# One array width for float32 products: products in halves, zero-filled tiles, paired heads and later-planned DMA consumers in an attention and FFN kernel

## The chip, the cores and the metric

The kernel runs on one core of a Trainium2 chip. The metric is the time on the device in microseconds (us). TensorE is PE in the rows, VectorE is DVE, ScalarE is ACT, GpSimd is POOL, and SyncE (SP) issues all DMAs here.

## The reference

Block-causal attention over 8 batches and 8 heads of 576 tokens and 64 dimensions; the heads side by side (512 columns) go through a feed-forward network (FFN) of 2048 hidden units.

```python
scores = scale * np.matmul(q, k.transpose(0, 1, 3, 2))
mask = pos[:, None] // 64 >= pos[None, :] // 64
scores = np.where(mask, scores, -1e9)
attn = softmax(scores)                       # rows
x = np.matmul(attn, v).transpose(0, 2, 1, 3).reshape(4608, 512)
h = x @ w_in                                 # 512 x 2048
g = h * np.clip(h + 3.0, 0.0, 6.0) / 6.0
out = g @ w_out                              # 2048 x 512
```

## The kernel before

q, k and v arrive as float32. The weights arrive as float64, seen as pairs of 32-bit words; they are made float32 on the chip (`w_load`), then scaled and split into a high and a low float16 part (`w_split`, tiles `win` and `wout`). Most products run on such pairs: high by high, high by low, low by high.

Two heads form a slot `n`; 32 slots, four for each batch. Blocks of 64 queries form groups `g` of three. TensorE's array of 128x128 is used in two widths. Float16 products are written as two halves of 64 output partitions (`h` = 0 and 1), each on 64 columns of the array, which run side by side ("128*64" in the rows, rows by columns of the array in use). Float32 products and all transposes take the whole width ("128*128").

The first batch (slots 0 to 3) has a path of its own in float32, which needs no scales:

- `qk_prep32` transposes q and k on TensorE (`qf`, for the last 192 tokens `qr`, into PSUM tiles `qt`), and lays q out so that one product gives the scores of both heads.
- `s_block32` makes the scores of a block (`sf`), takes their maximum (`st`) and the exponential (`pf` in SBUF); `t_block32` transposes that (`pt`) and copies it into `pT`.
- `pv_group32` spreads the reciprocal sums over the partitions with a product (`pr`, weights `halves`) and multiplies by V (`pf` in PSUM, from `vnat`), one head in each half of the array.
- `ffn1_f32` and the branch `pc == 0` of `ffn2_` are the float32 FFN of the first 384 tokens: `h0_f` and `o0_t`, for 16 hidden tiles f and three row tiles t.

`pow2_scale` finds a power of two over all partitions: it transposes the maxima (`mt`), reduces them, spreads the result over a small diagonal (`dg`) and multiplies by ones (`mb`). Maxima of V (`mt_v`) and of the weights (`mt_w`) take that path. In several places a tile has 64 rows or fewer: the last tokens of a slot in `qr`, the last block of a group in `pt` and `pT`, the last `j` of P V, and `dg` with one or two rows.

The order of all engines is made when the program is built. `Recorder` takes down every operation with a key (a planned time from tables such as `AS`, `RT`, `AT`, `FT`), its tiles and its possible engines (`scaled` lists them: A is ACT, V is DVE, P is POOL). `schedule` simulates the engines from a cost model and takes at each step, among the operations that are ready, the one with the lowest key. For TensorE an operation is `half` or not, and the planner keeps to one width while it can; a change of width costs `TURN`. `joint` keeps instructions together as one operation. `emit` then writes the operations in that order; all of them go through one line of the source (L470), so the rows of the profile are told apart by tile names. Nothing of the plan's times is in the program: an engine waits only for data and free tiles.

```python
            op.half = eng == "tensor" and outs[0].ap[0][1] <= 64 and method == "matmul"
```

Of the kernel before, what the change touches and what calls it, by code (L numbers as in the profile page):

```python
# [10 lines left out]
F32 = mybir.dt.float32  # L11
# [14 lines left out]
U = 1.598  # L26
AS = (7.023, 12.523, 17.83, 23.72)
AL = 18.177
PV0 = 2.73
TA, TR, PR = 2.293, 5.661, 0.564  # L30
QR = 2.65
PVA, PVB = 0.915, 0.993
# [6 lines left out]
EVP = 1  # L39
# [4 lines left out]
QL = -1.069  # L44
VL = -0.957
W0, WD = 22.454, 2.893
S0, SD = 55.334, 3.899
M0, MD = 34.048, 7.213
RT = (32.208, 42.3, 52.129, 62.298)
RS, RL, VL1 = 2.174, 27.037, 23.187  # L50
VM0, VMX = 40.792, 0.335
AT = ((4, 86.25), (6, 128.63), (8, 163.76), (9, 178.32), (10, 200.19), (12, 240.58), (14, 288.15), (16, 335.0), (24, 568.52), (32, 811.01))
FT = ((0, 34), (1, 120), (2, 165.14), (3, 234.43), (4, 274.43), (5, 349.43), (7, 498.87), (10, 739.05), (13, 984.05))
UNI = False
QP = 0.55
VP = 0.469
# [5 lines left out]
class Op:  # L62
# [3 lines left out]
    __slots__ = ("ways", "key", "preds", "joint", "n", "start", "end", "tiles", "eng", "half", "queue")  # L66
# [15 lines left out]
ADV = {("tensor", "a"): 99.36}  # L82


class Recorder:
# [76 lines left out]

    def add(self, ways):
# [56 lines left out]
    def cost(self, eng, method, args, kw, outs, ins):  # L220
# [46 lines left out]
        occ = max(n / 2.37, 26) * (4 if f32 else 1) + 2  # L267
        if f32 and method == "matmul":
            occ = max(occ, 200)
# [6 lines left out]
    def schedule(self):  # L276
# [63 lines left out]
        while done < N:  # L340
# [38 lines left out]
            else:  # L379
# [4 lines left out]
                for i, (key, k, rd) in enumerate(a):  # L384
                    h = ops[k].half
                    if not h and False in first:
                        continue
                    r = room(ops[k], t, full)
                    if r is None:
                        first.setdefault(h, i)  # L390
# [48 lines left out]
            margin = {}  # L439
            if o.queue:  # L440
                lead, tail, work = o.queue
                dma = max(t + lead, dma) + work
                o.end = dma + tail
                margin = self.MARGIN
            now[e] = t + occ
            self.busy[e] += occ
            for x in o.tiles:
                left[x] -= 1
                if not left[x]:
                    tag = self.meta[x][0]  # L450
                    free[tag].append(o.end + 60.0)
                    need[tag][head:span[x][1]] -= 1
# [21 lines left out]
def kernel(  # L474
# [65 lines left out]
    def pow2_scale(mx, n, nm, to=None, exact=False):  # L540
# [8 lines left out]
        if exact:  # L549
            pt_ = ps_s.tile([P, 512], F32, tag="s", name=f"mt_{nm}")  # L550
            nc.tensor.transpose(pt_[:n, :P], mx, ident)
            dg = sm.tile([P, n + 1], F32, tag=f"dg{n}", name=f"dg_{nm}")
            nc.vector.tensor_reduce(dg[:n, n:], pt_[:n, :P], axis=AX.X, op=ALU.max)
            nc.vector.tensor_scalar_mul(dg[:n, :n], ident[:n, :n], dg[:n, n:])
            mx, k_ = dg[:n, :n], n
        else:
            k_ = P
        ps = ps_s.tile([P, 512], F32, tag="s", name=f"mb_{nm}")
        nc.joint = "mb", nm
        for h in range(2):  # L560
            nc.tensor.matmul(ps[h * BLK:(h + 1) * BLK, :n], ones[:k_, :BLK], mx, start=True, stop=True)
# [261 lines left out]
    def qk_load32_rest(n):  # L823
        t = attp.tile([P, 2, NTR, 2, D], F32, tag="vhl", bufs=2, name=f"qr{n}")
        for s, src in enumerate((q, k)):
            nc.sync.dma_start(t[:, s, 0], src[0, 2 * n:2 * n + 2, T0:T0 + P].rearrange("h p d -> p h d"))
            nc.sync.dma_start(
                t[:BLK, s, 1], src[0, 2 * n:2 * n + 2, T0 + P:].rearrange("h p d -> p h d")
            )
        qn[n] = t  # L830

    def qk_prep32(n, rest):
# [28 lines left out]
        pss = []  # L861
        for s in (1, 0):
            if rest and not QTH:
                ps = ps_s.tile([P, 512], F32, tag="s", name=f"qt{n}_{s}r")
            else:
                ps = ps_h.tile([P, T0], F32, tag="h", name=f"qt{n}_{s}")
            for u in range(NTR if rest else NTA):
                m = min(P, c1 - c0 - u * P)
                nc.tensor.transpose(
                    ps[:, u * P:u * P + m], t[:m, s, u].rearrange("p h d -> p (h d)"),  # L870
                    ident[:m, :m],
                )
            pss.append(ps)
        nc.scaled(kT[:, c0:c1], pss[0][:, :c1 - c0], 1.0, "AV")
# [15 lines left out]
    def s_block32(n, i):  # L890
# [39 lines left out]
    def t_block32(n, i):  # L930
# [5 lines left out]
        half = nk % P and ii == GB - 1  # L936
# [10 lines left out]
        for u0 in range(0, nu, 4):  # L947
            u1 = min(u0 + 4, nu)
            full = u1 - 1 if half and u1 == nu else u1
# [5 lines left out]
            for u in range(u0, u1):  # L955
                m = P if u < full else BLK
                nc.tensor.transpose(pp[:m, u - u0], pr[:, u * P:u * P + m], ident)
            for a, e, m in ((u0, full, P), (full, u1, BLK)):
                if a < e:
                    dst = t[:m, ii * NU[g] + a:ii * NU[g] + e]  # L960
                    src = pp[:m, a - u0:e - u0]
                    nc.scaled(dst, src, 1.0, "AV")
            n_ev.append(1)

    def pv_group32(n, g):
# [16 lines left out]
        nc.tensor.matmul(pr, halves, rd.rearrange("p i x -> p (i x)"), start=True, stop=True)  # L982
# [7 lines left out]
        for j in range(nj):  # L990
            i0 = max(0, 2 * j - 3 * g)
            kp = BLK if 2 * j + 1 > 3 * g + 2 else P
            a = i0 * NU[g] + j
            us = slice(a, a + (GB - 1 - i0) * NU[g] + 1, NU[g])
            for h in range(2):
                nc.tensor.matmul(
                    ps[h * D:(h + 1) * D, i0 * BLK:],
                    vnat[n % NVB][:kp, j, h, :],
                    t[:kp, us, h * BLK:(h + 1) * BLK],
                    start=(j == 0),  # L1000
                    stop=(j == nj - 1),
                )
        if g < G32:
# [513 lines left out]
```

## Time and profile before

| | us |
|---|---|
| median of 3 runs | 1009.13 (1006.89 to 1009.73) |
| profiled execution | 1009.89 |
| its span | 1008.1 |
| PE busy | 988.0 (98%) |
| DVE busy | 765.2 (76%) |
| ACT busy | 691.5 (69%) |
| POOL busy | 23.7 (2%) |

The span runs from the first to the last instruction of the profiled execution. The granted clock of TensorE is 0.999 of full speed. Rows of operations in order of time give a start and a length; the length of a product holds a tail in which the next one already runs, so distances between starts tell what a product costs.

### The profile page before, as it was taken

What the parts mean: (1) busy time and instruction counts of PE and PEld (TensorE: products, weight loads), DVE (VectorE), ACT (ScalarE), POOL (GpSimd) and SP (SyncE); (2) the same over time, 40 slices, a digit from 0 to 9 for tenths busy, and PEclk for the clock granted to TensorE, in tenths of its full rate; (3) what the DMA queues carried; (4) which work ended last, traced back from release to release, by engine and by line L of the source; (5) the groups of instructions that cost most, each with busy time, mean ns of one, the idle gap of its engine ahead of it and who ended that gap; (6) DMA issues with size and microseconds to landing.
All of it is one profiled execution on the core that took longest, in us unless ns stands there. A gap on an engine that the chain in (4) does not pass through costs nothing. (4 is left out here: it accounts for less than half of the span.)

```text
span 1008.1 us, 28569 instructions
## 1 busy us (share of the span) xinstructions
PE 988.0 (98%) x11492; PEld 712.6 (71%) x11492; DVE 765.2 (76%) x2107; ACT 691.5 (69%) x1821; POOL 23.7 (2%) x98
## 2 busy tenths in 40 slices
PE   7999999999999999999999999999999999999998
PEld 5655544777767777777667767776777777777776
DVE  5899989899999899989999899689797532333332
ACT  5889876778878787888888787688776432333332
POOL 2000100000000000000000000000000000000000
PEclk9999999999999999999999999999999999999999
DMA  6786756989899888998899887778455300000000
GB/s 151 207 246 206 187 111 123 173 156 173 151 173 188 144 154 172 154 190 161 155 181 179 158 172 150 129 138 150 81 109 97 59 33 1 1 33 2 33 2 33
DMA packets 414197, 128.87 MB, mean 128 GB/s; under 512 B 403184, under 2 KB 403440, under 8 KB 414064
## 3 DMA queue, kind: packets, MB, share of 16 engines
q1 hardware_dynamic: 414064, 127.05, 64.2%
q8 instruction: 90, 1.47, 0.6%
q14 instruction: 43, 0.35, 0.1%
HBM read 45.09 MB, written 9.44 MB: 54 GB/s over the span
## 5 line engine op out<-in xcount | busy, mean ns | idle before, releaser
L470 PE MATMUL h<-x,win 128*64 128x384 f16 (+2 forms) x4720 | 440.0, 317 | 3.7 <-DVE r L470 2.8
L470 PE MATMUL o<-wout,g 128*64 128x512 f16 (+2 forms) x3348 | 432.4, 379 | 0.0
L470 PEld LDWEIGHTS <-win 128*64 128x64 f16 x4608 | 289.1, 110 | 71.7 <-issue 7.4
L470 PEld LDWEIGHTS <-g 128*64 128x64 f16 x3264 | 213.0, 110 | 96.1 <-DVE g L470 0.4
L470 ACT ACTIVATE r<-h,eg,sh 128x192 f32<-128x192 f32 (+1 forms) x240 | 134.2, 580 | 122.8 <-PE h L470 120.1
L470 DVE SCALAR_TENSOR_TENSOR r<-r,eg,h 128x384 f32<-128x384 f32 (+1 forms) x192 | 110.5, 576 | 133.9 <-ACT r L470 133.5
L470 ACT ACTIVATE p<-s,st,esc 128x64 f32<-128x64 f32 (+1 forms) x280 | 163.4, 587 | 16.4 <-DVE ph L470 6.4
L470 DVE SCALAR_TENSOR_TENSOR g<-r,g 128x384 f16<-128x384 f32 (+1 forms) x192 | 99.6, 520 | 34.7 <-ACT g L470 33.7
L470 DVE TENSOR_REDUCE st<-s 128x1 f32<-128x64 f32 (+1 forms) x280 | 117.7, 447 | 7.8 <-PE s L470 7.4
L470 ACT ACTIVATE g<-r 128x384 f16<-128x384 f32 (+1 forms) x151 | 74.3, 492 | 61.6 <-DVE r L470 60.8
L470 PE MATMUL s<-qkT 128*64 128x64 f16 (+7 forms) x1120 | 100.0, 288 | 3.5 <-ACT p L470 1.6
L470 PEld LDWEIGHTS <-qkT 128*64 128x64 f16 x1120 | 58.8, 110 | 35.7 <-issue 17.0
L470 PEld LDWEIGHTS <-vhl 128*64 128x64 f16 x1680 | 72.7, 110 | 14.4 <-issue 7.7
L470 PE MATMUL pv<-pT,vhl 128*64 128x192 f16 (+2 forms) x1680 | 73.8, 233 | 2.0 <-ACT p L470 0.8
L470 DVE SCALAR_TENSOR_TENSOR ph<-p,st,ph 128x256 f16<-128x256 f32 (+2 forms) x168 | 67.4, 445 | 0.0
L470 DVE SCALAR_TENSOR_TENSOR phl<-p,st,phl 128x512 f16<-128x512 f32 (+1 forms) x84 | 62.6, 789 | 0.0
L470 ACT ACTIVATE st<-st,esc 128x1 f32<-128x1 f32 (+2 forms) x127 | 36.7, 291 | 34.5 <-DVE st L470 33.6
L470 ACT ACTIVATION_READ_ACCUMULATOR p<-s,st,esc 128x1 f32 x280 | 55.1, 197 | 0.0
L470 ACT ACTIVATE ph<-p,st 128x192 f16<-128x192 f32 (+5 forms) x102 | 43.6, 468 | 7.4 <-DVE st L470 4.9
L470 ACT ACTIVATE qks<-qk 128x576 bf16<-128x576 f32 x56 | 37.9, 680 | 11.5 <-DMA qkT<-qks 11.5
L470 DVE SCALAR_TENSOR_TENSOR qks<-qk,rs_q,qks 128x576 f16<-128x576 f32 x56 | 43.7, 809 | 0.0
L470 DVE TENSOR_REDUCE vmax<-vnat 128x1 f32<-128x640 f32 x32 | 25.9, 808 | 5.7 <-DMA vnat<-in_v_dram 5.7
(158 smaller groups left out, 836.5 us busy)
## 6 DMA issues: line engine op xcount, KB each, us to landing
out_dram<-osb SPq DMA_DIRECT2D x35, 256.0 KB, 2.7
vnat<-in_v_dram SPq DMA_DIRECT2D x64, 128.0 KB, 2.9
qk<-in_q_dram SPq DMA_DIRECT2D x28, 288.0 KB, 3.6
qk<-in_k_dram SPq DMA_DIRECT2D x28, 288.0 KB, 4.2
rawi<-in_moe_w_in_dram SPq DMA_DIRECT2D x8, 512.0 KB, 4.5
rawo<-in_moe_w_out_dram SPq DMA_DIRECT2D x8, 512.0 KB, 4.5
ph<-in_moe_w_in_dram SPq DMA_DIRECT2D x6, 512.0 KB, 4.6
ph<-in_moe_w_out_dram SPq DMA_DIRECT2D x6, 512.0 KB, 4.1
```

Of the source, the lines that this page charges most:

```text
L470: getattr(eng, method)(*args, **kw)
```

## The change

- A new call `product` records a float32 product once, with a second form (`alt`): two halves of 64 output partitions, written one after the other. Its width is open (`half` is None), and the planner takes the form of the width that TensorE is in. `s_block32`, `pr`, `h0` and `o0` use it.
- Tiles of 64 rows become whole with zeros: `pr` in SBUF has 640 columns, whose tail POOL sets to zero; `t_block32` transposes and copies whole tiles; P V always takes 128 rows of V (whose tail is zero). The rest of q and k is loaded as three tiles, the middle one half q and half k, and gives three transposes in one PSUM bank instead of four in two.
- `mt` is a product in two halves (the maxima as weights, repeated over 64 columns, by the identity) instead of a transpose, and `dg` and `mb` use all 128 partitions.
- The two heads of a step of P V are one operation (`joint`).
- The planner's model (its unit is ns): changes of width cost 92 to half and 120 to full, with 95 more for an operation that begins a visit to full width; consumers of a DMA on every engine are planned 900 later (1250 on TensorE as before), a tile that a DMA frees comes free 900 later, results that TensorE uses come 100 later; unit costs of products are set anew. The tables of keys are new.

```diff
-MARGIN = {"tensor": 1250.0}
+LATE = {"tensor": 100.0}
+MARGIN = {"tensor": 1250.0, "vector": 900.0, "scalar": 900.0, "gpsimd": 900.0, "sync": 900.0}
+SLACK = 900.0
-TURN = 95
+TURN = {True: 92.0, False: 120.0}
+LOADS = 95.0
...
+    def product(self, out, w, x, **kw):
+        self.add([("tensor", "matmul", (out, w, x), kw)])
+        r = BLK
+        op = self.ops[-1]
+        op.half = None
+        op.alt = [
+            ("matmul", (out[h * r:(h + 1) * r], w[:, h * r:(h + 1) * r], x), kw) for h in range(2)
+        ]
...
-            if e == "tensor" and o.half != half:
-                half = o.half
-                self.turns += 1
-                t += self.TURN
+            if e == "tensor":
+                if o.half is None:
+                    if half:
+                        o.ways[e] = o.alt, occ, took, shared
+                elif o.half != half:
+                    half = o.half
+                    self.turns += 1
+                    t += self.TURN[half]
+                    if not half:
+                        occ += self.LOADS
+                        took += self.LOADS
...
-            margin = {}
+            margin, slack = self.LATE, 60.0
...
-                margin = self.MARGIN
+                margin, slack = self.MARGIN, 60.0 + self.SLACK
...
-                    free[tag].append(o.end + 60.0)
+                    free[tag].append(o.end + slack)
...
-            nc.tensor.transpose(pt_[:n, :P], mx, ident)
+            nc.joint = "mt", nm
+            for h in range(2):
+                wide = mx[:, h % n:h % n + 1].to_broadcast([P, BLK])
+                nc.tensor.matmul(pt_[h * BLK:(h + 1) * BLK, :P], wide, ident, start=True, stop=True)
+            nc.joint = None
...
-            kp = BLK if 2 * j + 1 > 3 * g + 2 else P
...
+            nc.joint = "pf", n, g, j
             for h in range(2):
                 nc.tensor.matmul(
                     ps[h * D:(h + 1) * D, i0 * BLK:],
-                    vnat[n % NVB][:kp, j, h, :],
-                    t[:kp, us, h * BLK:(h + 1) * BLK],
+                    vnat[n % NVB][:, j, h, :],
+                    t[:, us, h * BLK:(h + 1) * BLK],
...
-            nc.tensor.matmul(
+            nc.product(
                 ps, w_f32("i", c, d // 2)[:, d % 2, l], x32[:, d, :T0], start=(d == 0), stop=(d == NDT - 1)
             )
...
+                nc.product(a, g[:, c0:c1], w32, start=first, stop=last)
...
-RT = (32.208, 42.3, 52.129, 62.298)
+RT = (29.488, 39.58, 49.409, 59.423)
```

What stands where now. First TensorE about 13 us into the kernel before: scores of slot 1 (`sf1`), P V of slot 0 (`pf0_0` from `pT0` and `vnat0`), transposes (`pt0`, `pt1`), the spread sums (`pr0`). The last numbers are output partitions by columns; x2 is two equal instructions in a row. Before:

```order
L470 MATMUL pf0_0_151<-pT0_0_117,vnat0_100 64x192
L470 MATMUL sf1_0_0_134<-qkf1_124 128x128
L470 MATMUL sf1_1_0_141<-qkf1_124 128x128
L470 MATMUL pt0_4_0_152<-ident_91,pf0_4_138 128x128 x2
L470 MATMUL pr0_0_149<-rd0_0_148,halves_97 128x192
L470 MATMUL pt0_4_0_152<-ident_91,pf0_4_138 128x128
L470 MATMUL pf0_0_151<-pT0_0_117,vnat0_100 64x192
```

With the change:

```order
L491 MATMUL pf0_0_152<-pT0_0_117,vnat0_100 64x192 x2
L491 MATMUL sf1_0_0_134<-qkf1_124 64x128 x2
L491 MATMUL sf1_1_0_141<-qkf1_124 64x128 x2
L491 MATMUL pr0_0_150<-rd0_0_149,halves_97 64x192 x2
L491 MATMUL pf0_0_152<-pT0_0_117,vnat0_100 64x64 x2
L491 MATMUL pt0_4_0_155<-ident_91,pf0_4_138 128x128 x3
```

The two heads of `pf0_0` stand together; the scores and the spread sums behind them are in halves of 64 partitions, and the transposes come in a group after them.

TensorE in the middle of the float32 FFN: `h0` and `o0`, scores `sf3` of the first batch, maxima of the weights (`mt_w`, `mb_w`). Before:

```order
L470 MATMUL h0_6_477<-x0_81,win_85 128x384 x2
L470 MATMUL sf3_7_0_472<-qkf3_0_200,qkf3_2_202 128x512
L470 MATMUL sf3_8_0_481<-qkf3_0_200,qkf3_2_202 128x320
L470 MATMUL mt_w4_465<-ident_91,wm4_463 2x128
L470 MATMUL h0_6_477<-x0_81,win_85 128x384
L470 MATMUL o0_2_396<-wout_86,g0_3_393 128x512
L470 MATMUL sf3_8_1_482<-qkf3_0_200,qkf3_2_202 128x256
L470 MATMUL o0_0_394<-wout_86,g0_4_419 128x512
L470 MATMUL o0_1_395<-wout_86,g0_4_419 128x512
L470 MATMUL mb_w4_467<-dg_w4_466,one_98 64x2 x2
L470 MATMUL h0_7_489<-x0_81,win_85 128x384
```

With the change:

```order
L491 MATMUL mt_w4_484<-ident_91,wm4_482 64x128 x2
L491 MATMUL o0_1_394<-wout_86,g0_4_427 64x512 x2
L491 MATMUL o0_2_395<-wout_86,g0_4_427 64x512 x2
L491 MATMUL pr3_2_499<-rd3_2_498,halves_97 64x192 x2
L491 MATMUL mb_w4_486<-dg_w4_485,one_98 64x2 x2
L491 MATMUL h0_8_531<-x0_81,win_85 64x384 x4
L491 MATMUL mt_w5_514<-ident_91,wm5_512 64x128 x2
L491 MATMUL h0_8_531<-x0_81,win_85 64x384 x4
L491 MATMUL o0_0_393<-wout_86,g0_5_461 64x512 x2
L491 MATMUL mb_w5_516<-dg_w5_515,one_98 64x2 x2
```

Where products of 128 partitions took turns with `mb_w` of 64, everything is of 64 partitions, `mt_w` too.

DVE where the weights of one chunk are split: `rsio` holds the scales, a TENSOR_SCALAR on `win` makes the high part, a SCALAR_TENSOR_TENSOR on `win` with `rsio` the low one. Before:

```order
L470 TENSOR_SCALAR rsio_90<-pwio_89 128x2
L470 TENSOR_TENSOR rb1_2_408<-pf1_2_409,rb1_2_408 128x192
L470 RECIPROCAL rsio_90<-rsio_90 128x2
L470 TENSOR_SCALAR sgi5_0_469<-rawi5_0_468 128x512
L470 TENSOR_SCALAR win_85<-win_85,rsio_90 128x2x256
L470 SCALAR_TENSOR_TENSOR x1_82<-rb1_2_408,rs_v0_207,x1_82 128x192
L470 TENSOR_REDUCE st2_7_413<-sf2_7_0_414 128x1
```

With the change:

```order
L491 TENSOR_SCALAR rsio_90<-pwio_89 128x2
L491 SCALAR_TENSOR_TENSOR win_85<-exi5_0_430,sgi5_0_429 128x512
L491 SCALAR_TENSOR_TENSOR wout_86<-exo3_1_370,sgo3_1_369 128x512
L491 RECIPROCAL rsio_90<-rsio_90 128x2
L491 TENSOR_REDUCE st3_6_450<-sf3_6_0_451 128x1
L491 SCALAR_TENSOR_TENSOR win_85<-win_85,rsio_90 128x2x256 x2
L491 TENSOR_SCALAR sgi4_0_376<-ph1_88 128x512
```

The high parts stand on ACT or POOL there, and DVE makes the two low parts one after the other. In all, DVE makes 1 high part of `win` and `wout` (11 before), ACT 23 (16) and POOL 8 (5).

More of the change, by code (lines that the diff above doesn't have):

```diff
@@ L24 @@
 WY = 27
[L26 to L32, printed above, removed]
+U = 1.592
+AS = (6.899, 12.918, 18.225, 24.115)
+AL = 17.759
+PV0 = 2.584
+TA, TR, PR = 2.701, 5.502, 1.15
+QR = 2.616
+PVA, PVB = 1.013, 0.991
 PHS = 18
@@ L38 @@
 EVR = 3
-EVP = 1
+EVP = 4
 PRO = True
@@ L62 @@
 class Op:
-    __slots__ = ("ways", "key", "preds", "joint", "n", "start", "end", "tiles", "eng", "half", "queue")
+    __slots__ = ("ways", "key", "preds", "joint", "n", "start", "end", "tiles", "eng", "half", "queue", "alt")
 class Engine:
@@ L266, in cost @@
         f32 = mybir.dt.size(ins[0].dtype) == 4
-        occ = max(n / 2.37, 26) * (4 if f32 else 1) + 2
+        occ = max(n / 2.4, 26) * (4 if f32 else 1) + (5 if f32 else 2.7)
         if f32 and method == "matmul":
-            occ = max(occ, 200)
+            occ = max(occ, 90 if n <= 2 else 200)
         if method == "transpose":
@@ L385, in schedule @@
                     h = ops[k].half
-                    if not h and False in first:
+                    if not h and False in first and (h is False or True in first):
                         continue
@@ L389, in schedule @@
                     if r is None:
-                        first.setdefault(h, i)
+                        for m in (True, False) if h is None else (h,):
+                            first.setdefault(m, i)
                         if h:
@@ L823, in qk_load32_rest @@
     def qk_load32_rest(n):
[L824 to L829, printed above, removed]
+        t = attp.tile([P, 3, 2, D], F32, tag="vhl", bufs=2, name=f"qr{n}")
+        for dst, src, t0, t1 in (
+            (t[:, 0], q, T0, T0 + P), (t[:BLK, 1], q, T0 + P, S),
+            (t[BLK:, 1], k, T0, T0 + BLK), (t[:, 2], k, T0 + BLK, S),
+        ):
+            nc.sync.dma_start(dst, src[0, 2 * n:2 * n + 2, t0:t1].rearrange("h p d -> p h d"))
         qn[n] = t
@@ L860, in qk_prep32 @@
         c0, c1 = (T0, S) if rest else (0, T0)
[L861 to L865, printed above, removed]
-                ps = ps_h.tile([P, T0], F32, tag="h", name=f"qt{n}_{s}")
[L867 to L874, printed above, removed]
+        if rest:
+            ps = ps_s.tile([P, 512], F32, tag="s", name=f"qt{n}_r")
+            for u in range(3):
+                nc.tensor.transpose(ps[:, u * P:(u + 1) * P], t[:, u].rearrange("p h d -> p (h d)"), ident)
+            pss = ps[:, GT:2 * GT], ps[:, :GT]
+        else:
+            pss = []
+            for s in (1, 0):
+                ps = ps_h.tile([P, T0], F32, tag="h", name=f"qt{n}_{s}")
+                for u in range(NTA):
+                    nc.tensor.transpose(
+                        ps[:, u * P:(u + 1) * P], t[:, s, u].rearrange("p h d -> p (h d)"), ident
+                    )
+                pss.append(ps)
+        nc.scaled(kT[:, c0:c1], pss[0], 1.0, "AV")
         i, ie = c0 // BLK, c1 // BLK
@@ L955, in t_block32 @@
             for u in range(u0, u1):
[L956 to L962, printed above, removed]
+                nc.tensor.transpose(pp[:, u - u0], pr[:, u * P:(u + 1) * P], ident)
+            nc.scaled(t[:, ii * NU[g] + u0:ii * NU[g] + u1], pp[:, :u1 - u0], 1.0, "AV")
             n_ev.append(1)
@@ L981, in pv_group32 @@
             pr = ps_s.tile([P, GT], F32, tag="s", name=f"pr{n}_{g}")
-        nc.tensor.matmul(pr, halves, rd.rearrange("p i x -> p (i x)"), start=True, stop=True)
+        nc.product(pr, halves, rd.rearrange("p i x -> p (i x)"), start=True, stop=True)
         rb = sm.tile([P, GT], F32, tag="rb", bufs=2, name=f"rb{n}_{g}")
@@ L1295, in ffn2_ @@
                 w32 = w_f32("o", f // 2, f % 2).rearrange("p r l n -> p (r l n)")
-                if c1 - c0 == P:
-                    nc.tensor.matmul(a, g[:, c0:c1], w32, start=first, stop=last)
-                    continue
-                for h in range(2):
-                    nc.tensor.matmul(
-                        a[h * BLK:(h + 1) * BLK, :DM // 2], g[:, c0:c1],
-                        w32[:, h * DM // 2:(h + 1) * DM // 2], start=first, stop=last,
-                    )
+                nc.product(a, g[:, c0:c1], w32, start=first, stop=last)
                 continue
```

45 lines of the change are left out of this document (21 added, 24 removed).

## Prediction

> **What bounds the kernel now.** I read the page's first lines, then busy time by stretches, then TensorE's waits.
>
> ```profile
> span 1008.1 us, 28569 instructions
> PE 988.0 (98%) x11492; PEld 712.6 (71%) x11492; DVE 765.2 (76%) x2107; ACT 691.5 (69%) x1821; POOL 23.7 (2%) x98
> ```
>
> TensorE is busy 988.0 us of 1008.1; no other engine is near that.
>
> ```profile
> core 0: us, PE busy (x) PEld busy (x) DVE busy (x) ACT busy (x) POOL busy (x), PEclk, DMA share, GB/s
> 0.00:60.00 60.00, 52.82 (x287) 34.89 (x288) 43.96 (x137) 43.31 (x133) 9.89 (x37) 1.00 0.72 191
> 60.00:140.00 80.00, 80.00 (x394) 42.16 (x393) 77.40 (x218) 68.52 (x172) 5.81 (x8) 1.00 0.73 193
> 140.00:200.00 60.00, 59.71 (x639) 35.38 (x639) 51.52 (x160) 41.79 (x115) 0.77 (x5) 1.00 0.79 141
> 200.00:650.00 450.00, 442.30 (x6092) 334.30 (x6089) 412.02 (x1172) 361.94 (x1000) 6.05 (x40) 1.00 0.91 165
> 650.00:1008.00 358.00, 353.19 (x4093) 265.85 (x4087) 180.27 (x424) 175.91 (x403) 1.21 (x8) 1.00 0.27 54
> ```
>
> The columns are the stretch and its length, then busy us of PE, weight loads, VectorE (DVE), ScalarE (ACT) and GpSimd (POOL). PE idles 7.2 us in the first 60 us, then not at all up to 140 us. From 200 to 650 us it idles 7.7 us. DVE is nearly as full as PE between 60 and 140 us: 77.4 of 80.
>
> ```profile
> PE qt L470 <- DMA qf<-in_q_dram: 4.2, 1, 4.2
> PE h L470 <- DVE r L470: 2.8, 3, 1.5
> PE s L470 <- ACT p L470: 1.6, 2, 0.8
> PE s L470 <- DVE am_q L470: 1.5, 1, 1.5
> ```
>
> The longest wait of PE is the first load, which the change leaves. Everything else is a few short waits, so what counts is how long PE's own stream is, and "busy" hides gaps between instructions. The order of instructions in time shows those:
>
> ```profile
> 121.01 2.74 PE L470 MATMUL o<-wout,g 128*128 128x512 f32 x6
> 123.59 0.27 PE L470 MATMUL mt_w<-ident,wm 128*2 128x128 f32 x1
> 123.70 2.75 PE L470 MATMUL h<-x,win 128*128 128x384 f32 x8
> 126.28 1.88 PE L470 MATMUL o<-wout,g 128*128 128x512 f32 x4
> ...
> 169.38 0.93 PE L470 MATMUL h<-x,win 128*64 128x192 f16 x18
> 170.25 1.12 PE L470 MATMUL o<-x,g 128*128 128x512 f32 x2
> 171.30 0.44 PE L470 MATMUL h<-x,win 128*64 128x192 f16 x6
> 171.67 1.12 PE L470 MATMUL o<-x,g 128*128 128x512 f32 x2
> ```
>
> The columns are start, length (the last tail included), operation, count. A float32 product is two records here. Three products of 128x512 on the full array take 123.59 - 121.01 = 2.58 us, 0.86 each; the four of 128x384 that follow `mt` take 126.28 - 123.70 = 2.58, 0.645 each, or 0.16 per pass and 192 columns. Between products on half the array (128*64) one takes 171.30 - 170.25 = 1.05, so 0.19 more. The half-array work pays too: 18 halves take 0.87 and six take 0.37, so a pair costs 0.50/6 = 0.083 and 0.12 is left over at the change of width. Going to full width and back for a float32 product costs **0.31 us**.
>
> ```profile
> 65.23 0.60 PE L470 MATMUL pt<-ident,pf 128*128 128x128 f32 x4
> 65.67 0.48 PE L470 MATMUL qt_1r<-ident,qr 128*128 128x128 f32 x2
> 66.07 1.12 PE L470 MATMUL o<-wout,g 128*128 128x512 f32 x2
> ...
> 283.85 0.27 PE L470 MATMUL mt_v<-ident,vm 128*1 128x128 f32 x1
> 284.05 0.84 PE L470 MATMUL o<-wout,g 128*64 128x512 f16 x6
> ```
>
> Four transposes of 128 rows take 0.44, 0.11 each. The two of `qt_1r`, of which one has 64 rows, take 0.40 where 0.22 would do: going to fewer rows and back costs 0.18 as well, 0.09 each way. The transpose `mt_v` takes 0.20 when half-array work follows, against 0.11 for `mt_w` above: 0.09 for the way back, so 0.12 + 0.09 = 0.21 for a visit that begins with transposes.
>
> **The change part by part.** Changes of width or rows, counted in PE's order of both kernels: 160 before, 21 after. Of the 160, 120 are width and 40 rows alone; after it none is rows alone. Visits to full width that begin with a float32 product fall from 41 to none. I divide at the second tile of the first hidden layer (`h0_1`, near 60 us) and at the last `o0` (near 174 us).
>
> *Up to 60 us:* width changes 34 to 12, 11 visits fewer: 8 x 0.31 + 3 x 0.21 = 3.1 us; row changes 11 x 0.09 = 1.0. Heads of P V:
>
> ```profile
> 20.73 0.54 PE L470 MATMUL pf<-pT,vnat 128*64 128x192 f32 x2
> 21.20 0.33 PE L470 MATMUL pt<-ident,pf 128*128 128x128 f32 x1
> ```
>
> A head alone takes 21.20 - 20.73 = 0.47, less 0.09 for the change of width 0.38. A pair shares the array, as the next rows show, and needs two passes of 0.16 = 0.32 for both. Five pairs are split before and none after: 5 x 0.32 = 1.6. The transposes of q and k fall from four to three for each of two head pairs (-0.2), and `mt`, which was one transpose of 0.11, becomes a product of two passes of 128 columns, about 0.22, twice here (+0.2). Together -5.7.
>
> *60 to 174 us:* width changes 74 to 9, all of those gone begun by products: 32.5 x 0.31 = 10.1; rows 16 x 0.09 = 1.4; transposes -0.2; eight `mt` +0.9. Together -10.8.
>
> *Later:* six visits for `mt_v` x 0.21 = 1.3, rows 13 x 0.09 = 1.2, six `mt` +0.7. Together -1.8.
>
> Half-array float32 must cost no more than full for this to hold:
>
> ```profile
> 62.77 1.78 PE L470 MATMUL pf<-pT,vnat 128*64 128x192 f32 x20
> 64.48 0.91 PE L470 MATMUL h<-x,win 128*128 128x384 f32 x2
> ...
> 246.59 2.14 PE L470 MATMUL o<-wout,g 128*64 128x512 f16 x18
> 248.53 0.26 PE L470 MATMUL mb_q<-qkmx,one 128*64 128x2 f32 x4
> 248.61 0.69 PE L470 MATMUL h<-x,win 128*64 128x384 f16 x6
> ```
>
> Twenty records of `pf`, 16 of 192 columns and 4 of 64, in pairs, take 1.71: 8 x 0.16 = 1.3 plus two short passes of about 0.1 plus changes of 0.2. So a pair runs at the full array's rate. And `mb_q`, float32 on the half array between float16 halves, takes 0.08 with no gap: the type alone costs nothing.
>
> The sum of PE's stream is -18.3 us. What of it reaches the end? Up to 60 us PE, DVE (44.0 of 60) and ACT (43.3 of 60) take turns in chains from load to P V; I count half, -2.9, between 0 and -5.7. From 60 to 174 us PE waits for nothing, but DVE must follow: it has 2.6 us to spare up to 140 us, and its splits of the weights fall from 11 to 1 in its order.
>
> ```profile
> L470 DVE TENSOR_SCALAR win<-win,rsio 128x512 f16<-128x512 f32 x7 | 3.8, 540 | 0.0
> ```
>
> Ten of 0.54 are 5.4 us less for DVE, which goes to ACT (7 more, 68.5 of 80 busy) and POOL (3 more). With 2.6 that is 8.0 of room against 10.8 x 80/114 = 7.6 of gain, just enough; I take off 1.5 for waits, leaving -9.3. The later -1.8 I take whole.
>
> The planner's numbers (margins behind DMAs, slots freed later, class keys) put no wait into the program; they sort it. I price the new order at 0, between -2 and +3: some of the 7.7 us of idle after 200 us could go, or as much come. The small edits:
>
> ```profile
> L470 POOL MEMSET pf<- 128x64 f32 x12 | 1.8, 153 | 38.7 <-PE pt L470 38.5
> ...
> L470 ACT ACTIVATE pT<-pt 64x128 f32<-64x128 f32 x8 | 2.1, 264 | 0.5 <-PE pt L470 0.5
> ```
>
> POOL sets eight more tails of `pf` to zero, 8 x 0.153 = 1.2 us on an engine that is 2% busy; uncovered, each delays one transpose by 0.15. ACT loses four evictions of 64 rows into `pT`, 4 x 0.264 = 1.1 us, about what two or three of its new splits cost. Reductions and scalings of `dg` keep their column counts.
>
> ```profile
> qk<-in_q_dram SPq DMA_DIRECT2D x28, 288.0 KB, 3.6
> rawo<-in_moe_w_out_dram SPq DMA_DIRECT2D x8, 512.0 KB, 4.5
> ```
>
> ```profile
> PE pv L470 <- DMA pT<-ph: 0.6, 1, 0.6
> ```
>
> SP issues 423 DMAs as before, but the four `qr2` loads pass `vnat4` and the `qk4` and `qk5` loads, and the raw weights `rawo0_1` pass two of these. A load that is passed lands later by at most another's time to landing, 3.6 to 4.5 us. After the first load, the longest wait of PE for a DMA is this one of 0.6 for a transposed tile, so a later load is hidden; if not, it is one such landing. What is late next is DVE between 60 and 140 us.
>
> Sum: -2.9 - 9.3 - 1.8 = -14.0, so a span of 994.1. The profiled execution took 1009.89, 1.8 more than its span, and lies 0.8 over the median of 1009.13: 994.1 + 1.8 - 0.8 = 995.1. Ends: all 18.3 and 2 of idle give 989; the next paragraph gives 1003.
>
> **Rivals.** *DVE or ACT sets the pace.* If the moved splits do not help, 60 to 140 us gives only DVE's 2.6, the 34 us behind it 10.8 x 34/114 = 3.2, the end 1.8, the start nothing: 7.6, so 1001.5, to 1003 with some new waits. For it: 77.4 of 80. Against: the 5.4 us that leave DVE; and in PE's new order the first scores of the second batch (`s4_0`) stand behind eleven tiles of `h0` instead of seven, which takes attention's reductions out of this stretch. [...]
>
> *POOL's splits come late.* The order has four splits of `win` in a row on POOL.
>
> ```profile
> L470 POOL TENSOR_SCALAR win<-win,rsio 128x512 f16<-128x512 f32 x2 | 4.1, 2067 | 25.4 <-DVE sums L470 20.1 <-DVE rsio L470 5.3
> ```
>
> At 2.07 each the fourth is done 8.3 us after the first starts, and the FFN's half-array products of the first float16 piece need them. Fully exposed that takes 8.3 from 14.0: 1003.4. It becomes a loss only over 3.5 us each. Against: PE has other pieces' work by then.
>
> *Slower: loads of half-width float32 weights are not hidden.* A product in halves has four loads, not two.
>
> ```profile
> L470 PEld LDWEIGHTS h<-x,win 128*128 128x128 f32 x112 | 19.2, 190 | 12.1 <-issue 2.7 <-DVE x L470 1.0 <-DVE vmax L470 0.4
> ...
> L470 PEld LDWEIGHTS pf<-pT,vnat 128*64 128x64 f32 x128 | 8.8, 136 | 6.5 <-issue 1.5 <-ACT pT L470 1.3 <-DVE pT L470 1.0
> ```
>
> A full-width load takes 190 ns, a 64-column one 136. 109 products go in halves (43 of `h0`, 44 of `o0`, 14 `sf`, 8 `pr`). If each pays two extra loads, 2 x 0.136 x 109 = 29.7: 1009.1 - 14.0 + 29.7 = 1025; the sign turns at 14.0/109 = 0.13 us, one exposed load. Against: `pf` above, 1.71. [...]
>
> [...]
>
> **How the numbers follow.** Forecast (989 to 1000, likeliest 995): 0.66. DVE's or ACT's pace (1000 to 1005): 0.18. POOL late or other new waits up to the whole gain: 0.07, of which half ends within 0.3% (1006.1 to 1012.2, about what a measurement can tell from no change) and half just below. Exposed loads: 0.05, slower. Nothing: 0.02, same. The last 0.02: new waits over the gain. So faster 0.87, same 0.06, slower 0.07. The range 988 to 1003 leaves out what lies over 1003.
>
> **What would show it.** Right: `o0` and `h0` as 128*64 float32, two of an `o0` product's four records starting together, 0.86 per product between half-array neighbours; no `pt` or `qt` after about 105 us; PE's span from 60 us to the last `o0` about 9 us shorter; the last 350 us unchanged in length. Wrong: rows of `h0` that start over 0.65 us apart per product; PE idle in 60 to 140 us with DVE named as releaser (the second case) or POOL `win` (the third); more idle between 200 and 650 us than 7.7, which would mean that the new order costs.

## The result and the profile after

The changed kernel takes 983.64 us (median of 4 runs, 982.83 to 984.63) against 1009.26 us (4 runs, 1006.89 to 1009.73): a ratio of 0.9751, 95% interval 0.9734 to 0.9769. The direction was forecast, the size was not: the gain is 25.6 us where 14.0 were expected, and the time lies 4.4 us below the range. The profiled execution took 982.83 us, its span 981.0, so the spans differ by 27.1; the profiled execution of before was 0.6 above its median, that of after 0.8 below.

The page's first lines, then busy time by the same stretches as before (us of PE, weight loads, DVE, ACT, POOL; granted clock; DMA):

```profile
span 981.0 us, 29087 instructions
PE 964.2 (98%) x11754; PEld 722.9 (74%) x11754; DVE 756.4 (77%) x2081; ACT 696.5 (71%) x1840; POOL 28.3 (3%) x109
...
0.00:60.00 60.00, 55.15 (x383) 40.23 (x385) 47.22 (x142) 48.89 (x151) 9.44 (x43) 1.00 0.79 211
60.00:140.00 80.00, 80.00 (x573) 39.17 (x571) 79.01 (x240) 70.98 (x174) 11.02 (x14) 1.00 0.72 186
140.00:200.00 60.00, 58.20 (x930) 44.25 (x927) 55.97 (x167) 50.15 (x146) 0.91 (x6) 1.00 0.94 163
200.00:650.00 450.00, 444.06 (x6110) 348.79 (x6111) 411.84 (x1160) 368.59 (x1012) 5.75 (x38) 1.00 0.92 164
650.00:981.00 331.00, 326.83 (x3772) 250.43 (x3767) 162.33 (x375) 157.94 (x361) 1.21 (x8) 1.00 0.26 54
```

PE is as full as before, in a shorter span. Its idle time between 200 and 650 us is 5.9 us, where it was 7.7. DVE is busy 79.0 of 80 us between 60 and 140 us, and still PE does not stop there. Its waits:

```profile
PE h L491 <- DVE r L491: 4.4, 3, 2.0
PE qt L491 <- DMA qf<-in_q_dram: 3.9, 1, 3.9
PE s L491 <- ACT p L491: 1.3, 2, 1.1
PE pv L491 <- DMA pT<-ph: 0.9, 2, 0.5
```

The products of the first batch in PE's order of time (start, length, operation, count):

```profile
122.66 0.51 PE L491 MATMUL s<-qkT 128*64 128x384 f16 x4
122.98 1.90 PE L491 MATMUL o<-wout,g 128*64 128x512 f32 x8
124.70 0.62 PE L491 MATMUL s<-qkT 128*64 128x512 f16 x4
125.13 1.04 PE L491 MATMUL o<-wout,g 128*64 128x512 f32 x4
125.99 2.12 PE L491 MATMUL h<-x,win 128*64 128x384 f32 x12
127.92 0.37 PE L491 MATMUL s<-qkT 128*64 128x448 f16 x2
```

A product in halves has four records. Two of `o` take 124.70 - 122.98 = 1.72 us, 0.86 each; three of `h` take 127.92 - 125.99 = 1.93, 0.643 each. Those are the full array's times, and nothing is added where float16 meets float32.

**Where the time came from.** For this I give each record of PE the time that equal records take when they stand back to back (a float32 product of 384 columns 0.645 us, as above; a transpose 0.109), sum these, and call what the clock shows beyond the sum PE's *lag*. The sums are 950.4 us before and 951.8 after: the work is 1.4 us longer, which is what the prediction's terms for `mt` and the transposes add up to. The lag fell. The last two columns are experiments that keep one kernel's order (below):

| lag in us at | before | after | order of after, products whole | order of before, products in halves |
|---|---|---|---|---|
| 60 us | 18.9 | 9.9 | 13.1 | 17.9 |
| 140 us | 26.0 | 11.5 | 21.0 | 22.8 |
| 200 us | 33.2 | 14.4 | 27.0 | 27.7 |
| 250 us | 36.8 | 16.6 | 29.3 | 29.8 |
| 650 us | 49.9 | 23.8 | 37.3 | 44.5 |
| 950 us | 53.4 | 25.3 | 38.9 | 47.6 |

So -9.0 us came up to 60 us, -9.8 from 60 to 200, and -9.3 after 200; with +1.4 of work that is -26.7 of the span's -27.1. The prediction had -2.9, -10.0 and -2.5 for these (its +1.4 of work left out).

After 200 us I also counted the gaps of over 0.13 us between two records of PE at the same width and rows: 37 gaps with 16.7 us before, 13 with 9.0 after. That is -7.7; changes of width and rows there went from 3.4 us to none, and smaller gaps grew by about 1.8.

### The profile page after: what moved, and what is told of

Same layout as the page of the kernel before. It is cut to its first block, busy times and chain, and to the rows that moved or that the text cites. A ratio compares the mean times of both kernels' runs of the same rounds, so it can differ in the third digit from the quotient of the medians.

```text
span 981.0 us, 29087 instructions
## 1 busy us (share of the span) xinstructions
PE 964.2 (98%) x11754; PEld 722.9 (74%) x11754; DVE 756.4 (77%) x2081; ACT 696.5 (71%) x1840; POOL 28.3 (3%) x109
## 4 chain that ended last, share of the span: by engine, by line
PE 58%; DVE 6%; DMA 2%; ACT 1%; issue 1%; DVEq 0%; ACTq 0%
PE o L491 25%; PE h L491 25%; PE s L491 4%; PE pv L491 4%; DMA pT<-ph 2%; DVE st L491 1%; DVE phl L491 1%; DVE ph L491 1%; DVE r L491 1%; DVE g L491 1%; DVE qks L491 1%; DVE vhl L491 0%; ACT p L491 0%; DVE x L491 0%; ACT r L491 0%
## 5 line engine op out<-in xcount | busy, mean ns | idle before, releaser
L491 PE MATMUL h<-x,win 128*64 128x384 f16 (+3 forms) x4790 | 440.7, 319 | 4.4 <-DVE r L491 4.4
L491 PEld LDWEIGHTS <-win 128*64 128x64 f16 x4608 | 296.1, 110 | 62.5 <-issue 6.5
L491 PEld LDWEIGHTS <-g 128*64 128x64 f16 x3264 | 219.2, 110 | 91.6
L491 ACT ACTIVATE p<-s,st,esc 128x64 f32<-128x64 f32 (+1 forms) x280 | 163.1, 586 | 13.6 <-DVE ph L491 7.3
L491 ACT ACTIVATE g<-r 128x384 f16<-128x384 f32 (+1 forms) x157 | 77.4, 494 | 59.2 <-DVE r L491 58.7
L491 PEld LDWEIGHTS <-qkT 128*64 128x64 f16 x1120 | 62.0, 110 | 23.5 <-issue 7.6
L491 ACT ACTIVATE st<-st,esc 128x1 f32<-128x1 f32 (+2 forms) x127 | 36.8, 291 | 34.3 <-DVE st L491 32.9
L491 ACT ACTIVATE ph<-p,st 128x64 f16<-128x64 f32 (+5 forms) x106 | 43.2, 450 | 15.8 <-DVE st L491 14.2
L491 DVE SCALAR_TENSOR_TENSOR qks<-qk,rs_q,qks 128x576 f16<-128x576 f32 x56 | 44.5, 807 | 0.1
L491 ACT ACTIVATE x<-pv 128x192 f16<-128x192 f32 (+1 forms) x56 | 20.3, 363 | 11.5 <-PE pv L491 10.0
```

Source lines behind the costliest of these rows:

```text
L491: getattr(eng, method)(*args, **kw)
```

## The experiments

Two questions: is a visit to full width worth 0.31 us (theory S: what the stream loses is gained in full, and is nearly all of the gain), or does the new order give most of it by fewer waits (theory O)? And if the order does, what in it: the tables, the pairs, the narrow tiles, the planner's margins behind DMAs (theory D), its margin on results that TensorE uses (theory L), or the course of the plan as such? Nine of the kernels are planned anew, two keep an order. All are set against runs of the kernel before on the same chip, whose medians were 1007.8 to 1008.1 us. "200 to 250" is the lag gained in that stretch. "Over" below is the distance to the changed kernel's 983.64 us. That was measured in another set, in which the kernel before took 1.1 to 1.5 us more than in these, so "over" is uncertain by about that much.

| kernel | changes of width or rows | median us | ratio to before (95%) | 200 to 250 |
|---|---|---|---|---|
| before | 160 | 1009.26 | | 3.6 |
| after | 21 | 983.64 | 0.9751 (0.9734 to 0.9769) | 2.2 |
| order of after, products whole | 105 | 997.41 | 0.9897 (0.9882 to 0.9912) | 2.3 |
| order of before, in halves | 111 | 1004.21 | 0.9962 (0.9948 to 0.9976) | 2.1 |
| products whole, planned anew | 91 | 996.45 | 0.9889 (0.9860 to 0.9917) | 5.8 |
| margins and slack of before | 27 | 994.26 | 0.9876 (0.9843 to 0.9910) | 10.4 |
| tables of before | 31 | 987.54 | 0.9805 (0.9775 to 0.9835) | 7.1 |
| before with the new margins | 144 | 1005.89 | 0.9983 (0.9971 to 0.9996) | 10.0 |
| heads of P V apart | 33 | 994.94 | 0.9875 (0.9855 to 0.9895) | 8.3 |
| narrow tiles of before | 81 | 991.21 | 0.9842 (0.9820 to 0.9865) | 2.1 |
| no `LATE` | 27 | 988.09 | 0.9811 (0.9785 to 0.9837) | 4.9 |
| no DMA margins | 21 | 996.18 | 0.9895 (0.9869 to 0.9920) | 11.9 |
| `LATE` of 200 | 25 | 985.21 | 0.9786 (0.9761 to 0.9811) | 4.7 |

**Float32 products whole, planned anew.**

```diff
-        op.half = None
+        op.half = False
```

> The changed kernel with every float32 product kept at the full width (the planner may not put it in halves); zero-filled tiles, paired heads, margins and tables stay. PE's order then has 91 changes of width in place of 21, 40 of the visits begun by a float32 product. Theory S (what the change gives is PE's stream, at the prediction's prices): 40 x 0.31 = 12.4 less five visits begun by transposes, so about 11 us more than the changed kernel, 995. Theory O (the new order gives most of it, by fewer waits): clearly less than 11, 986 to 990, since order and margins stay.

996.45 us, 12.8 over the changed kernel, near what S has: 40 visits begun by a product came back, 40 x 0.31 = 12.4, less about 1 for five visits begun by transposes, so 11.4. But the plan moved too (5.8 us lost between 200 and 250 us where the changed kernel loses 2.2), so the agreement alone does not settle the price. The run with a fixed order below does.

**The planner's margins of before.**

```diff
-    LATE = {"tensor": 100.0}
-    MARGIN = {"tensor": 1250.0, "vector": 900.0, "scalar": 900.0, "gpsimd": 900.0, "sync": 900.0}
-    SLACK = 900.0
+    LATE = {}
+    MARGIN = {"tensor": 1250.0}
+    SLACK = 0.0
```

> The changed kernel with the planner's margins of before: no 100 ns for results that TensorE uses, 1250 ns behind a DMA for TensorE alone, no later freeing of tiles; tables, halves and zero-filled tiles stay. PE's stream stays (27 changes of width against 21: +0.9). Theory S: 984 to 985. Theory O with the margins as its cause: the roughly 8 us of waits that went after 200 us and some of the start's come back, 990 to 993, and the gaps stand in the stretch from 200 to 650 us. Theory O with the tables as its cause: 984 to 985 here and the loss in the kernel with old tables.

994.26 us, 10.6 over, and a little beyond the 990 to 993 of theory O with the margins as its cause. TensorE's stream is only 1 us longer, and the lag is 16.2 at 200 us against 14.4; nearly everything is lost between 200 and 250 us, where TensorE's granted clock is at half for 6.83 us (0.93 on average from 200 to 250 us; last section). The margins put no wait into the program and still carry about 10 us.

**The tables of before.** The block of numbers from `U` to `VP`, and `ADV`, are those of before; the rest is the changed kernel.

> The changed kernel with the tables of keys of before (U to VP and the lead of attention on TensorE); margins, halves, zero-filled tiles stay. 31 changes of width, stream +1.5. Theory S: 985. Theory O with the tables as its cause: 990 or more, above all in the first 60 us, where the tables moved the last third of the first batch 3 us earlier.

987.54 us, 3.9 over: between the 985 of theory S and the 990 of theory O, so it decides for neither. Here too the clock is at half for 6.83 us from 207.8 us on (0.83 on average from 200 to 220 us).

**The kernel before with the new margins.**

```diff
-    MARGIN = {"tensor": 1250.0}
+    LATE = {"tensor": 100.0}
+    MARGIN = {"tensor": 1250.0, "vector": 900.0, "scalar": 900.0, "gpsimd": 900.0, "sync": 900.0}
+    SLACK = 900.0
```

> The kernel before with the changed kernel's margins alone (100 ns for results that TensorE uses, 900 behind a DMA on every other engine and for tiles that a DMA frees). 144 changes of width or rows against 160, stream -2.5. Theory S: 1006 to 1007. Theory O with the margins as its cause: 8 us or more faster, 998 to 1001.

1005.89 us, some 2 us better than before and close to theory S. So the margins that carry 10 us in the changed kernel carry 2 here. This plan has 42 gaps after 200 us (18.1 us), no fewer than before's 37: the margins alone do not remove them. Some of the gaps stand in 10.24 us at the half clock, from 218.2 us on (0.90 on average from 200 to 250 us).

**Heads of P V apart.**

```diff
-            nc.joint = "pf", n, g, j
+            nc.joint = None
```

> The changed kernel with the two heads of a step of P V as two operations again, which the planner may part. 33 changes of width against 21 (+1.5). Theory S: the split pairs cost 0.32 each and the width +1.5, so 985 to 987. Theory O (the start's gain comes from chains that close earlier, not from the stream): lag at 60 us, 9.9 us in the changed kernel, is back above 14 and the time 988 or more.

994.94 us, 11.3 over; lag and time are those of theory O. Up to 60 us the lag is 14.5 instead of 9.9, so 4.6 us belong to that stretch. Another 6 are lost between 200 and 250 us, long after the last P V of the first batch. PE's waits from 200 to 220 us, and busy time around the longest:

```profile
PE h L491 <- DVE x L491: 3.1, 1, 3.1
PE h L491 <- ACT x L491: 1.5, 1, 1.5
```

```profile
212.00:216.00 4.00, 0.93 (x13) 0.74 (x14) 3.02 (x6) 1.84 (x6) 0.00 (x0) 0.68 0.78 182
216.00:220.00 4.00, 3.75 (x31) 2.31 (x28) 3.02 (x9) 2.94 (x10) 0.00 (x0) 0.50 0.97 185
```

The third number from the end is the granted clock: it falls in the wait and is 0.50 after it.

**Narrow tiles as before** (`mt` as a transpose with `dg` and `mb` of one or two rows; the 64-row tails of `pt`, `pT` and P V; `pf`'s last tail not zeroed).

> The changed kernel with the narrow tiles of before (mt a transpose, dg and mb of one or two rows, pT, pt and the last step of P V of 64 rows; the three whole transposes of the rest of q and k stay). 81 changes of width or rows, 43 of them of width, against 21. Theory S: 38 x 0.09 + 11 visits x 0.21 - 16 x 0.11 (the transposes are cheaper than the products) = +4.0, so 987 to 989. If a change of rows alone is free: 984 to 985.

991.21 us, 7.6 over and 2 to 4 more than expected. The lag is 2.6 us over the changed kernel's at 60 us, 7.9 at 200, and 3.9 more come between 250 and 650 us; the work is shorter by 1.4. Part of it is the price of a change of rows, which was put too low (below); part is a wait of 2.6 us for DVE that ends at 171.9 us, with 3.41 us at the half clock behind it.

**The two margins one by one.** Without `LATE`, and without the DMA margins and slack:

```diff
-    LATE = {"tensor": 100.0}
+    LATE = {}
```

> The changed kernel without the 100 ns that the planner adds for results of other engines that TensorE uses; the margins behind DMAs and of freed tiles stay. The kernel with all old margins lost 10.6 us, nearly all of it after 200 us. Theory L (small gaps on TensorE are what the margin removes): most of the 10.6 here, 990 or more. Theory D (consumers planned too close behind DMAs are what costs): 984 to 986 here.

988.09 us, 4.5 over: between the 984 to 986 of theory D and the 990 of theory L.

```diff
-    MARGIN = {"tensor": 1250.0, "vector": 900.0, "scalar": 900.0, "gpsimd": 900.0, "sync": 900.0}
-    SLACK = 900.0
+    MARGIN = {"tensor": 1250.0}
+    SLACK = 0.0
```

> The changed kernel with no margin behind a DMA on engines other than TensorE and no later freeing of tiles; the 100 ns for TensorE stay. Theory L: 984 to 986. Theory D: 990 or more, with a wait for a DMA on TensorE or just ahead of it between 200 and 250 us, and the granted clock below 1.0 there.

996.18 us, 12.5 over, with the same 21 changes of width. Of the new margins those behind DMAs carry most, as theory D has it, with the wait and the low clock that it expected. The profiled execution is the slowest of the four (999.52 us). Stretches of 4 us from 204 us on:

```profile
204.00:208.00 4.00, 2.14 (x36) 1.36 (x32) 2.86 (x10) 3.41 (x10) 0.00 (x0) 1.00 1.14 232
208.00:212.00 4.00, 1.22 (x16) 0.85 (x17) 3.49 (x9) 2.48 (x8) 0.00 (x0) 0.53 1.10 205
```

PE in order of time there, with the wait and its releaser in brackets; then the last step of that DMA's source `qks`, and the issuing queue of SP:

```profile
205.64 0.50 PE L491 MATMUL o<-wout,g 128*64 128x256 f16 x6
210.16 0.85 PE L491 MATMUL s<-qkT 128*64 128x64 f16 x12 [4.02 <-DMA qkT<-qks]
```

```profile
202.22 0.67 ACT L491 ACTIVATE qks<-qks 128x576 f16<-128x576 f16 x1
```

```profile
201.60 0.40 SPq L491 DMA_DIRECT2D qk<-in_q_dram  x1
202.06 1.39 SPq L491 DMA_DIRECT2D qk<-in_k_dram  x1
203.55 4.57 SPq L491 DMA_TRANSPOSE qkT<-qks  x1
```

SP issues the transposing DMA that PE needs at 206 only at 203.55 us; its issue takes 4.57 us. The loads of later tiles stand ahead of it in SP's queue, but they hold it by 0.7 us at most, because ACT finishes `qks` only at 202.89. In the changed kernel DVE finishes `qks` at 196.09, SP issues the DMA right behind it, and PE waits at most 1.6 us in that stretch:

```profile
195.57 0.52 DVE L491 TENSOR_SCALAR qks<-qks 128x576 f16<-128x576 f16 x2
```

```profile
196.16 4.83 SPq L491 DMA_TRANSPOSE qkT<-qks  x1
```

```profile
PE h L491 <- DVE r L491: 1.6, 1, 1.6
```

So what comes late is the work that feeds the DMA. I read this as what a margin behind a DMA does in a planner: it makes the planner count the consumer as late, so work that feeds it is taken earlier. No run shows that step of the planner by itself.

**The order of after, products whole.** To price the visits without a new plan, the order stays and only the form that is written out changes:

```diff
-                        o.ways[e] = o.alt, occ, took, shared
+                        pass
```

> The order of all engines is that of the changed kernel, instruction for instruction; only the float32 products that it emits in column halves are emitted whole. TensorE's changes of width or rows rise from 21 to 105, so there are 42 visits to the full width more, nearly all begun by a product. By the prediction's price of 0.31 us a visit that is 13.0 us: theory S (the price of a visit alone made the gain) expects 996 to 998, and that the lag that TensorE gathers after 200 us stays at the changed kernel's 9 us. The rival (much of what undoing the halves cost earlier was a new plan, and VectorE's pace covers part of the visits) expects 988 to 993.

997.41 us, 13.8 over. 42 visits, so 0.33 each (13.6 by the spans: 0.32), where 0.31 was predicted. All of them stand before 200 us, and the lag up to there is 12.6 us more than in the changed kernel, 0.30 each. Theory S holds for this part, and the rival with 988 to 993 falls. In order of time:

```profile
128.91 2.20 PE L491 MATMUL h<-x,win 128*128 128x384 f32 x6
131.04 0.52 PE L491 MATMUL s<-qkT 128*64 128x384 f16 x4
131.49 1.98 PE L491 MATMUL o<-wout,g 128*128 128x512 f32 x4
133.40 0.62 PE L491 MATMUL s<-qkT 128*64 128x512 f16 x4
133.96 1.13 PE L491 MATMUL o<-wout,g 128*128 128x512 f32 x2
```

Three products of `h` take 2.13 us where the halves took 1.93, two of `o` 1.91 where they took 1.72, and the four halves of 384 columns 0.45 where they took 0.32: 0.19 to 0.20 on one side of a visit, 0.13 on the other. These are the prices of this trace; what TensorE does in that time is not shown. After 200 us this kernel loses about what the changed one does (10.3 us against 9.4 up to 650 us; its profile has 3.41 us at the half clock there, from 307.7 us on).

**The order of before, products in halves** wherever the operation ahead on PE is on half the array; `product` is as in the change, with `half` left at full for the planner.

```diff
         for o in self.schedule():
+            if o.eng == "tensor":
+                if o.alt and half:
+                    o.ways["tensor"] = (o.alt, *o.ways["tensor"][1:])
+                else:
+                    half = o.half
```

> The order of all engines is that of the kernel before, instruction for instruction; a float32 product (sf, pr, h0, o0) is emitted in column halves wherever the product ahead of it on TensorE was on half the array. Width changes fall from 121 to 57 and none of the visits left begins with a float32 product; changes of rows alone rise from 39 to 54. By the prediction's prices the stream is 8.4 us shorter: if that is all, 999 to 1001. If the other engines, whose order was planned for the slower stream, hold TensorE back, 1002 to 1006. In both the lag that TensorE gathers after 200 us should stay at the kernel before's 17 us if the new order made the gain there, and fall to about 10 if the halves did.

1004.21 us: 3.6 us better than before on the same chip (the profiled spans, from different sets, differ by 6.2), where the stream is 8.4 shorter. The rival is right here: the other engines, in an order planned for a slower PE, give part of it back. Up to 200 us the lag falls by 5.5; after it the lag grows by 16.8 up to 650 us, as before (16.7). PE's waits between 60 and 200 us, where before had one of 0.3:

```profile
PE h L485 <- DVE r L485: 1.1, 1, 1.1
PE mb_q L485 <- DVE x L485: 0.5, 1, 0.5
PE s L485 <- DVE x L485: 0.3, 1, 0.3
PE s L485 <- ACT p L485: 0.2, 1, 0.2
```

The gaps after 200 us go with the order, not with the halves: 40 with 16.0 us here, 18 with 9.5 us in the order of after. This pair of runs settles that the gain after 200 us is not the halves'. The kernels in the order of after also have the whole tiles; but the changed kernel with narrow tiles, planned anew, has only 16 such gaps with 10.6 us, so I put this gain down to the order.

**A larger `LATE`**, since PE's longest waits left are for `r`:

```diff
-    LATE = {"tensor": 100.0}
+    LATE = {"tensor": 200.0}
```

> The changed kernel, planned with 200 ns instead of 100 for every result of another engine that TensorE uses. 25 changes of width, so the stream is 0.5 us longer. If the waits on VectorE's r (4.4 us) that are left go and nothing else moves, 979 to 982. If the new plan puts TensorE into the wait at about 205 us that the other new plans had, 987 to 992.

985.21 us, no better than the changed kernel. The lag gained between 200 and 250 us rises by 2.5, and from 250 to 650 us falls by 1.4. It is neither of the two cases that were expected.

## Why the prediction was wrong in size

**Right: the price of a visit.** 0.31 was predicted, 0.30 to 0.33 measured with the order fixed. Full-width visits begun by a product are the largest single part: 12.6 to 13.8 of the 25.6 us.

**Right: 60 to 174 us.** -9.3 was taken, about -10.0 without the extra work; up to 200 us the lag fell by 9.8. What was feared there did not come. DVE did fill up (79.0 of 80 us), so the margin of 8.0 us worked out for it was used, but PE's waits from 60 to 200 us come to 1.7 us. The mark that I gave for this, the time from 60 us to the last `o0`, can't be used: in the new order the last `o0` starts at 157.9 us. In the kernel before it starts at 178.8, not near 174 as the prediction read it, and there are 121 changes of width and 39 of rows alone, not 120 and 40. The last transposes of `pt` come at 92.6 us, as forecast.

**Wrong: half counted up to 60 us.** The step was "I count half, -2.9", because PE, DVE and ACT were said to take turns in chains there. Measured: -9.0, more than the whole term of 5.7. Busy time from 10 to 60 us, before and then after:

```profile
10.00:60.00 50.00, 47.67 (x271) 31.03 (x270) 40.23 (x125) 39.93 (x125) 3.23 (x10) 1.00 0.74 201
```

```profile
10.00:60.00 50.00, 49.80 (x365) 36.07 (x366) 43.33 (x128) 44.80 (x141) 2.63 (x15) 1.00 0.82 225
```

Once the first load is in, PE was busy 47.7 of 50 us and is now busy 49.8. In the new order it sets the pace there too; most of the 7.2 us of idle in the first 60 us lies before 10 us. DVE and ACT had room and did more in the same time. Of the -9.0 changes of width and rows make -6.4 (7.9 us at 45 changes before, 1.5 at 13 after), for which the step had 4.1; the rest is smaller gaps, waits and heads that stood alone. The chains were not imaginary: with the halves alone, in the order of before, the changes of width and rows up to 60 us cost about 2 us less and the lag there fell by 1.0. The step went wrong in carrying that half over to a new order with pairs and whole tiles. Two undone parts price pieces of it: 3.2 us with products whole in the same order, 4.6 with the heads apart, newly planned.

```profile
16.91 0.55 PE L491 MATMUL pf<-pT,vnat 128*64 128x192 f32 x4
17.29 0.50 PE L491 MATMUL pr<-rd,halves 128*64 128x192 f32 x4
17.61 0.39 PE L491 MATMUL sf<-qkf 128*64 128x128 f32 x4
17.83 0.71 PE L491 MATMUL pf<-pT,vnat 128*64 128x192 f32 x8
```

Paired heads, sums and scores of both slots now share one visit to half the array.

**Wrong: the new order at 0, between -2 and +3.** Measured: -7.7 us of gaps after 200 us. The two runs with a fixed order show that it is not the halves, and the narrow tiles bring little of it back, so it is the order's. Without the margins behind DMAs the changed kernel has 41 such gaps with 21.6 us (the half clock is in them), so they have a part in it. The bound was taken from PE's idle time between 200 and 650 us, 7.7 us. That was the wrong quantity: the gaps between PE's records at one width came to 14.5 us in the same stretch, since a busy time counts the tail of each product (1.90 us for the eight records of `o` at 122.98 us after, of which the next start comes 1.72 later). Taking the whole stream (-18.3) and these 7.7 gives -26.0 where the spans differ by 27.1.

**Too small: a change of rows.** 0.09 each was predicted; the excess at the 39 changes of rows alone in the kernel before sums to 5.8 us, 0.15 each. The later term of -1.8 falls short for the same reason: changes after 200 us cost 3.4, not 2.5.

**The rivals.** POOL's splits were no brake:

```profile
L491 POOL TENSOR_SCALAR win<-win,rsio 128x512 f16<-128x512 f32 x5 | 5.5, 1103 | 34.8 <-PE h L491 14.3 <-DVE win L491 10.7 <-DVE rsio L491 9.9
```

One takes 1.10 us on average, not the 2.07 of before, and PE's waits name no POOL. The loads of half-width float32 weights take 137 ns, where those of `pf` took 136 before, and are hidden: the rows of `o` and `h` above leave no room for them.

```profile
L491 PEld LDWEIGHTS o<-wout,g 128*64 128x64 f32 x152 | 10.5, 137 | 10.4 <-issue 10.1
```

**Open.** Why the margins bring 10 us in the changed kernel and 2 in the kernel before. The half clock is a part of the answer: it cost the kernel before with the new margins about 3.3 us, and the changed kernel with the old ones about 2.5 (last section). The rest is not shown. Each newly planned kernel changes its whole course after 200 us, and between 250 and 650 us alone the lag grows by 3.6 to 14.7 us among the thirteen kernels; no run isolates which table or margin makes a course good there. The undone parts add up to far more than the gain (12.8 + 10.6 + 3.9 + 11.3 + 7.6 = 46.2 against 25.6), which shows that they are not shares of it.

## What to carry to other kernels

Where TensorE's type and width vary, count its changes of width and multiply by the price of a round trip, here 0.30 to 0.33 us; a product that takes the width the array is in saves that, here at no cost in passes (0.86 us for an `o` of 512 columns in either form). In a kernel whose order is planned, an undone part is a new plan: fix the order and change only what is written out, or the price of the plan is read as the price of the edit. Read the granted clock of each run too: in seven of the nine new plans the half clock is a part of the price. And judge how full the bound engine is after its first data has come, by the gaps between its records, not by the listed waits.

## What the hardware showed that was not expected

Waits of TensorE cost more than themselves in eight of the thirteen traces: the granted clock (third from the end) goes to 0.50 ahead of the last 10 us, and stays there for 3.41 us or two, three or four times as long. Without the DMA margins PE stands from 206.1 to 210.2 us:

```profile
208.20:208.40 0.20, 0.00 (x0) 0.00 (x0) 0.10 (x1) 0.06 (x1) 0.00 (x0) 0.70 1.27 232
...
221.80:222.20 0.40, 0.40 (x17) 0.40 (x14) 0.40 (x2) 0.00 (x0) 0.00 (x0) 0.83 0.17 12
```

A mean of 0.70 over 208.20 to 208.40 puts the fall to 0.50 at 208.28, 2.2 us into the wait, and 0.83 over 221.80 to 222.20 the rise at 221.94: 13.66 us at half. With the heads apart, where waits of 1.5 and 3.1 us stand close together:

```profile
213.00:213.50 0.50, 0.00 (x0) 0.00 (x0) 0.50 (x2) 0.42 (x1) 0.00 (x0) 0.93 0.64 160
...
220.00:221.00 1.00, 1.00 (x17) 0.75 (x16) 0.46 (x4) 0.48 (x2) 0.00 (x0) 0.87 0.64 145
```

From 213.43 to 220.26, that is 6.83 us, half of the other. In the order of after with whole products, PE waits 2.1 us up to 306.81 us, and the clock falls when it is at work again:

```profile
307.60:307.80 0.20, 0.20 (x10) 0.20 (x7) 0.20 (x1) 0.20 (x2) 0.00 (x0) 0.72 1.17 218
...
311.00:311.20 0.20, 0.20 (x9) 0.20 (x7) 0.20 (x2) 0.20 (x2) 0.00 (x0) 0.75 0.10 9
```

From 307.69 to 311.10, that is 3.41 us.

In the 3.41 us ahead of the fall PE was busy for 1.27 us, 37%, without the DMA margins, where its work ends at 206.14 us. With the heads apart it was busy for 0.51 us, 15%, in these records:

```profile
209.35 0.83 PE L491 MATMUL pv<-pT,vhl 128*64 128x192 f16 x18
211.63 0.35 PE L491 MATMUL h<-x,win 128*64 128x384 f16 x2 [1.45 <-ACT x L491]
```

After its first load the changed kernel has waits of up to 2.0 us, and they leave the clock at 1.00 up to 979.52 us, when PE's work is over. The 3.41 us ahead of that fall are 33% busy, and those ahead of the last fall of the kernel before, at 1006.96 us, 22%. Between 10.3 us and the last 10 us, all at 1.00, PE is busy for at least 41% of any 3.41 us in the changed kernel (from 290.7 us on) and 55% in the kernel before (from 555.8 us on). The length of a wait does not decide by itself: without `LATE` waits of 0.9 and 1.4 us between 200 and 220 us come with a mean clock of 0.91 there, while with the products whole, planned anew, waits of 1.1 and 1.8 us in the same 20 us leave it at 1.00. That the work done in such a stretch decides is my reading; no run shows it by itself.

This is part of the price of most kernels that were planned anew. In their profiled executions the clock is at half for 3.41 us without `LATE` and with narrow tiles, 6.83 us with the margins of before, the tables of before and the heads apart, 10.24 us in the kernel before with the new margins, and 13.66 and 3.41 us without the DMA margins. At the half clock six records of `h` take 0.92 us up to the next start and at the full clock twelve take 0.98, so six 0.49, in the trace without the DMA margins:

```profile
219.42 1.17 PE L491 MATMUL h<-x,win 128*64 128x384 f16 x6
220.34 2.05 PE L491 MATMUL pv<-pT,vhl 128*64 128x192 f16 x30
222.19 1.17 PE L491 MATMUL h<-x,win 128*64 128x384 f16 x12
223.17 0.62 PE L491 MATMUL s<-qkT 128*64 128x512 f16 x4
```

The same work takes 1.88 times as long there, so the work that PE does in such a stretch, counted as for the lag, is about what the half clock costs: an estimated 1.7 to 1.8 us of 3.41, 2.4 to 2.5 of 6.83, 3.3 of 10.24 and 4.2 of 13.66.
